# Part of a first product by Strassen's scheme, and one batch of attention input pooled in another layout, in a fused attention and MLP kernel

## The chip, the cores and the metric

One core of one Trainium2 chip. The metric is device time in microseconds (us) of one execution; several executions are timed and medians given. Every run here used one core. A profile gives one execution's span (its first to its last instruction), which in these runs is 1.7 to 2.9 us less than the time of that run.

## The reference, cut to what matters

```python
# q, k, v: (8 batches, 8 heads, 576, 64);  w_in: (512, 2048);  w_out: (2048, 512)
k_p = k.reshape(B, H, 72, 8, 64).mean(axis=3)          # pooled keys, v_p likewise
scores = (1/8) * q @ k_p^T ; attn = softmax(scores) ; a = attn @ v_p
x = a.transpose(0, 2, 1, 3).reshape(4608, 512)
h = x @ w_in ; g = h / (1 + exp(-h)) ; out = g @ w_out
```

## The kernel before

The 4608 tokens go through nine stages of 512. Stage t has a first product ("up", hidden values = w_in x) and a second ("down"). The attention of batch t + 1 is woven in: a list of fillers, each with a step number, is worked off between the matmuls. `spread` emits a filler once that many steps have been issued.

```python
def up(t, fillers, items):                       # 16 column groups g of 128
    step = spread(fillers, len(items) * KF)      # KF = 4
    for g, n0, n in items:
        hp_ps = ps_tile([128, 512], FP32, "mm", "hp_ps")      # 3 banks
        ...
            next(step)
            nc.tensor.matmul(hp_ps[:, r0:r1], lhsT=w_in_sb[:, kk, g*128:(g+1)*128], rhs=xT[...])
        nc.scalar.activation(h_T[:, g, n0:n0+n], hp_ps[:, :n], func=AF.Silu)
```

Strassen's scheme replaces the eight block products of a 2 x 2 block product by seven, at the price of extra sums. The second product is already done so (P, Q, R are PSUM tiles, the sums of hidden quarters and of weight quarters are made on the Vector engine). In the first two batches the pooling uses rows: partition = (head, position), which needs a small selection product afterwards. From batch 2 on it uses a tree over tiles with one position per partition.

```python
def slot_sums(name, j):        # rows: 128 partitions, 3 or 2 slots; used for batches 0 and 1
    ...                        # adds of 768, 384, 192 (or 512, 256, 128) elements
def select_v(b, a):            # brings pooled rows into place; both halves a use one PSUM tile
    if a == 0:
        st["v_ps"] = ps_tile([128, H, D], FP32, tag, "v_ps")
    ...
def copy_v(b, a):              # Vector: vp[:, half a] = v_ps[:, half a]
def tree(dsts, raw):           # one position per partition; 72 partitions busy
    ...
# in stage t, with a = t + 1:
f_up.append((0, lambda: pool_k(a)))
if t == 1:                     # batch 2: two half trees per tensor, no accumulating load
    f_up.append((46, lambda: pool_v(a, (0,))))
    f_down.append((30, lambda: pool_heads(a, "v", 1)))
elif t:
    f_up.append((10, lambda: pool_v(a)))
```

The softmax here doesn't subtract the row's maximum and nothing guards it: scores larger than these inputs give would overflow.

Of the kernel before, what the change touches and what calls it, by code (L numbers as in the profile page):

```python
# [27 lines left out]
FP32 = mybir.dt.float32  # L28
FP32R = mybir.dt.float32r
BF16 = mybir.dt.bfloat16  # L30
AX = mybir.AxisListType.X
AF = mybir.ActivationFunctionType
# [4 lines left out]
def kernel(  # L37
# [9 lines left out]
    nc = tc.nc  # L47
# [42 lines left out]
    def ps_tile(shape, dtype, tag, name):  # L90
        return psum.tile(shape, dtype, tag=tag, bufs=banks[tag], name=name)
# [18 lines left out]
    t_sb = singles.tile([128, 2, CQ], FP32, name="t_sb")  # L110
    xT = singles.tile([128, KF, NX], BF16, name="xT")


    kz = [singles.tile([128, 2, 2, SP], BF16, name=f"kz{n}") for n in range(2)]
    gate = singles.tile([128, 1], FP32, name="gate")
# [40 lines left out]
    def raw_tile(tag, heads, full=False):  # L156
        raw = big.tile([128, H * PH], FP32, tag=tag, name="raw")
        if full:
            return raw
        return raw[:SP, : H * PH].rearrange("k (h e) -> k h e", h=heads)  # L160

    def source(b, name):
        return (k if name == "k" else v)[b].rearrange("h (sp p) d -> sp h (p d)", p=POOL)


    def load_rows(eng, out, in_):
        for r0, r1 in ((0, 64), (64, SP)):
            eng.dma_start(out=out[r0:r1], in_=in_[r0:r1])

    def load_one(b, name):  # L170
        st = batches.setdefault(b, {})
        raw = raw_tile(f"{name}_raw", H)
        load_rows(nc.sync, raw, source(b, name)[:, :, :PH])
        st[f"{name}_raw"] = raw

# [43 lines left out]
    def pool_heads(b, name, i):  # L219
        tree([pooled(b, name, i)], batches[b][f"{name}_raws"][i])  # L220
# [21 lines left out]
    def k_transpose(b, parts=(0, 1)):  # L242
        st = batches[b]
        kT_ps = ps_tile([128, 2, 2, SP], BF16, "at", "kT_ps")
        for a in parts:
            for c in range(2):
# [18 lines left out]
    SA = SLOTS - 1  # L265
    row_tiles = {
        n: [
            raw_tile(f"{n}_raw{i}", H, full=True)[:, : m * RE].rearrange(
                "r (i e) -> r i e", e=RE
            ) for i, m in (("", SA), (2, SLOTS + 1 - SA))  # L270
        ] for n in "kv"
    }

# [62 lines left out]
    def copy_v(b, a, copy=nc.vector.tensor_copy):  # L336
        hs = slice(4 * a, 4 * (a + 1))
        copy(out=batches[b]["vp"][:, hs, :], in_=batches[b]["v_ps"][:SP, hs, :])
# [68 lines left out]
    def spread(fillers, n):  # L407
        todo = sorted(fillers, key=lambda f: f[0])
        for i in range(n):
            yield i  # L410
            while todo and todo[0][0] <= i:
                todo.pop(0)[1]()
        for f in todo:
            f[1]()


    def up(t, fillers, items):
        step = spread(fillers, len(items) * KF)
        for g, n0, n in items:
            hp_ps = ps_tile([128, 512], FP32, "mm", "hp_ps")  # L420
            c0 = (t * NTT + n0) % NX

            for r0, r1 in ((0, min(n, NX - c0)), (min(n, NX - c0), n)):
                for kk in range(KF) if r1 > r0 else ():
                    if r0 == 0:
                        next(step)
                    x0 = (c0 + r0) % NX
                    nc.tensor.matmul(  # L428
                        hp_ps[:, r0:r1],
                        lhsT=w_in_sb[:, kk, g * 128 : (g + 1) * 128],  # L430
                        rhs=xT[:, kk, x0 : x0 + r1 - r0],
                        start=(kk == 0), stop=(kk == KF - 1),
                    )
            nc.scalar.activation(h_T[:, g, n0 : n0 + n], hp_ps[:, :n], func=AF.Silu)  # L434
        for _ in step:
            pass

    def store(t, m, cs, engines=(nc.sync,)):
        n0 = (t * NTT + m * 128) // QP
# [220 lines left out]
    load_slots(nc.gpsimd, 1, "v", 4, 5)  # L660
    load_w_out(3)

    visits = [(f, g) for f in range(2) for g in range(2)]
    for t in range(NT):
        a = t + 1
        f_up, f_down = [], []
        if t == 0:
            GA = 11
            items = [(g, 0, HS) for g in range(GA)]
            items += [(g, HS, NTT - HS) for g in range(GA)]  # L670
            items += [(g, 0, NTT) for g in range(GA, KG)]
            f_up += [(1, lambda: denominators(0, 0, 1, on_dve=True))]
            f_up += [(5, lambda: denominators(0, 1, 1, on_dve=True))]
            f_up += [(13, lambda: numerators(0, 0, 1))]
            f_up += [(17, lambda: numerators(0, 1, 1))]
        else:
            items = [(g, 0, NTT) for g in range(KG)]
            for n, k0, k1, at in (
                (6, 0, 4, 20), (6, 4, 8, 36),
                (2, 0, 4, 51), (5, 0, 4, 52), (1, 0, 4, 53), (2, 4, 6, 58), (5, 4, 6, 59),  # L680
            ):
                f_up.append((at, lambda n=n, k0=k0, k1=k1: hidden_sum(n, k0, k1)))
            f_up.append((64, lambda: hidden_sum(2, 6, 8)))
            f_up.append((64, lambda: hidden_sum(5, 6, 8)))
            f_up.append((64, lambda: hidden_sum(1, 4, 8)))
            f_down.append((27 if t < NT - 1 else 41, lambda: hidden_sum(7, 0, 8)))

        for n, t0, f_to, at in (
            (1, 0, f_down, 48), (3, 0, f_down, 54), (4, 1, f_up, 12),
            (7, 1, f_down, 10), (6, 1, f_down, 50),  # L690
        ):
            for i in range(PW):
                if t == t0:
                    f_to.append((at + i, lambda n=n, i=i: weight_sum(n, i)))
        if a < B:
            q_at = [20, 28, 36, 44] if t else [82, 84, 86, 88]
            if t == 0:
                for j in range(2):
                    f_up.append((44 + 8 * j, lambda j=j: slot_sums("k", j)))
                    f_up.append((72 + 8 * j, lambda j=j: select_k(1, j)))  # L700
                    f_up.append((72 + 8 * j, lambda j=j: copy_k(1, j)))
                    f_down.append((20 + 10 * j, lambda j=j: slot_sums("v", j)))
                    f_down.append((37 + 3 * j, lambda j=j: select_v(1, j, "at")))
                    f_down.append((37 + 3 * j, lambda j=j: copy_v(1, j)))
            else:
                f_up.append((0, lambda: pool_k(a)))
                f_up.append((25, lambda: k_transpose(a)))
            for n in range(4):
                f_up.append((q_at[n], lambda n=n: q_transpose(a, n // 2, n % 2)))
            if t == 1:  # L710
                f_up.append((46, lambda: pool_v(a, (0,))))
                f_down.append((30, lambda: pool_heads(a, "v", 1)))
            elif t:
                f_up.append((10, lambda: pool_v(a)))
            if t == 0:
                f_down.append((0, lambda: load_q(2)))

                last = w_out_sb[:SP, KG - 1, d_model - 1 :]
                f_down.append(
                    (1, lambda: load_heads(2, "k", ("k_raw", "k_raw2"), last))  # L720
                )
                f_down.append(
                    (14, lambda: load_heads(2, "v", ("v_raw", "v_raw2"), last))
                )
            elif a + 1 < B:
                f_v = f_up if t > 1 else f_down
                f_up.append((0, lambda: load_q(a + 1)))
                f_up.append((1, lambda: load_one(a + 1, "k")))
                f_up.append((2, lambda: load_rest(a + 1, "k")))
                f_v.append((11 if t > 1 else 31, lambda: load_one(a + 1, "v")))  # L730
                f_v.append((12 if t > 1 else 32, lambda: load_rest(a + 1, "v")))
            f_down.append((0, attn_tables))

            if t:
                sc_at, den_at, nu_at = (1, 28, 56, 77), (28, 46, 69, 89), (46, 69, 89, 93)
            else:
                sc_at, den_at, nu_at = (1, 14, 22, 30), (14, 22, 30, 38), (42, 47, 52, 57)
            for n, (f, g) in enumerate(visits):
                f_down.append((den_at[n], lambda f=f, g=g: denominators(a, g, f)))
                f_down.append((sc_at[n], lambda f=f, g=g: scores(a, g, f)))  # L740


            for n, (f, g) in enumerate(visits):
                if n < 3 or not 3 <= t < B - 2:
                    f_down.append((nu_at[n], lambda f=f, g=g: numerators(a, g, f)))
                if n == 0 and 3 < t < B - 1:
                    f_down.append((nu_at[n], lambda: numerators(a - 1, 1, 1)))
        moe_tables()
        up(t, f_up, items)
        if t == 0:  # L750
            down(t, f_down, [(0, 1, 2), (3,)])
        else:
            down_quarters(t, f_down, last=t == NT - 1)
# [28 lines left out]
```

## Time and profile before

| | before |
|---|---|
| time, first 3 runs / all 4 of the first comparison | 295.84 / 295.86 us |
| span, granted clock | 294.7 us, 0.997 |
| Tensor / Vector / Scalar busy | 98 / 65 / 60 % |
| stage 1 (up start to next up start) | 54.21 to 86.02 = 31.8 us |
| stages 2 to 7 | 30.6, 30.1, 30.5, 30.3, 30.8, 26.0 us |

Stage ends are read off the chain of waits, where a run of `hp_ps` follows a run of 16 `o_psQ`. "Granted clock" is the share of its full clock that the Tensor engine got. A Vector sum of 512 elements per partition takes 0.68 us there in fp32 (`rr_sb`) and 0.42 in bf16 (`w_sum`). The prediction shows the lines that matter; two more serve for comparison. First the one Tensor wait in the middle of the kernel, from the view of waits (total us, times, longest), then, from the chain, the up of stage 7, which has no attention beside it:

```profile
PE sc_ps L348 <- DVE xT L396: 0.7, 1, 0.7
...
238.30 13.81 PE hp_ps L428 x64
```

### The profile page before, as it was taken

To read this page: it belongs to the slowest core of one execution; us is meant where nothing else is said; L and a number is where in the kernel's file an instruction comes from. 1 tells how busy PE (TensorE), PEld (TensorE's weight loads), DVE (VectorE), ACT (ScalarE), POOL (GpSimd) and SP (SyncE) were. 2 spreads that over 40 slices of the span, in tenths; PEclk is the share of its full clock that TensorE was granted. 3 is DMA by queue.
4 is the path that set the end of the run, shared out by engine and by line. 5 is a ranking of instruction groups with operands and counts; after the bars stand their busy time and mean duration, and the time that the engine had idled before them with its cause. 6 is when DMAs were issued, how large, how long until landed. Compare 5 with 4: busy or idle time off the path is not lost.

```text
span 294.7 us, 6052 instructions
## 1 busy us (share of the span) xinstructions
PE 287.9 (98%) x2417; PEld 175.6 (60%) x2417; DVE 191.2 (65%) x344; ACT 177.6 (60%) x366; POOL 42.8 (15%) x60
## 2 busy tenths in 40 slices
PE   8999999999999999999999999999999999999995
PEld 3348434446564666457788774476547654884584
DVE  4886445999978566865586659666865642741562
ACT  1677675567566865676667675776577666407500
POOL 8654100001300120013001710110000000000000
PEclk9999999999999999999999999999999999999998
DMA  7999999958794797487857895783500032004003
GB/s 215 271 282 205 247 229 180 209 147 174 106 177 108 160 132 136 106 177 111 150 128 162 120 122 137 167 116 51 123 20 2 2 89 53 2 22 117 6 12 135
DMA packets 34909, 37.65 MB, mean 128 GB/s; under 512 B 9856, under 2 KB 26368, under 8 KB 34880
## 3 DMA queue, kind: packets, MB, share of 16 engines
q0 software_dynamic: 20128, 18.50, 37.3%
q1 hardware_dynamic: 14176, 17.84, 26.5%
q10 hardware_dynamic: 576, 0.92, 0.9%
q8 instruction: 19, 0.31, 0.5%
q14 instruction: 10, 0.08, 0.1%
HBM read 36.70 MB, written 9.44 MB: 157 GB/s over the span
## 4 chain that ended last, share of the span: by engine, by line
PE 86%; DVE 10%; ACT 1%; issue 1%; DVEq 0%
PE hp_ps L428 37%; PE o_psQ L535 14%; PE o_psP L535 14%; PE o_psR L535 4%; PE sc_ps L348 4%; PE o_ps L462 4%; PE warm_ps L583 4%; PE nu_ps L388 3%; DVE raw L197 3%; DVE h_sum L495 2%; PE den_ps L365 2%; DVE w_sum L513 2%; DVE qT L148 1%; DVE xT L396 1%; PE kz_ps L313 1%
## 5 line engine op out<-in xcount | busy, mean ns | idle before, releaser
L428 PE MATMUL hp_ps<-xT,w_in_sb 128*128 128x512 bf16 (+3 forms) x684 | 128.2, 345 | 0.4 <-ACT h_T L434 0.4
L434 ACT ACTIVATE h_T<-hp_ps 128x512 bf16<-128x512 f32 (+2 forms) x155 | 87.4, 567 | 57.4 <-PE hp_ps L428 45.3
L428 PEld LDWEIGHTS <-w_in_sb 128*128 128x128 bf16 x684 | 65.9, 98 | 56.6 <-issue 1.5
L495 DVE TENSOR_TENSOR h_sum<-h_T 128x1024 bf16<-128x1024 bf16 (+2 forms) x88 | 52.0, 637 | 36.1 <-ACT h_T L434 36.1
L535 PEld LDWEIGHTS <-h_sum 128*128 128x128 bf16 x640 | 60.9, 98 | 15.1 <-issue 6.5
L356 ACT ACTIVATE es<-sc_ps 72x288 bf16<-72x288 f32 x128 | 41.4, 403 | 13.2 <-PE sc_ps L348 13.1
L396 DVE TENSOR_TENSOR xT<-nu_ps,rec 128x288 bf16<-128x288 f32 x64 | 25.7, 448 | 12.0 <-PE nu_ps L388 11.8
L535 PEld LDWEIGHTS <-h_T 128*128 128x128 bf16 x256 | 23.6, 98 | 6.5 <-issue 4.1
L177 POOL DMA_DIRECT2D raw<-in_k_dram x5 | 7.1, 1420 | 114.5 <-DVE h_sum L495 48.4
L148 DVE STREAM_TRANSPOSE qT<-q_bf 128x576 bf16<-128x576 bf16 x32 | 23.6, 758 | 0.0
L374 ACT ACTIVATE lnd<-den_ps 128x288 f32<-128x288 f32 x30 | 12.3, 411 | 16.6 <-PE nu_ps L388 9.8
L197 DVE TENSOR_TENSOR raw<-raw 72x1024 f32<-72x1024 f32 (+1 forms) x18 | 19.7, 1094 | 0.1
L291 DVE TENSOR_TENSOR raw<-raw 128x768 f32<-128x768 f32 (+3 forms) x16 | 10.5, 654 | 11.1 <-DMA raw<-in_v_dram 7.8
L535 PE MATMUL o_psP<-w_out_sb,h_sum 128*128 128x256 bf16 x128 | 17.6, 273 | 0.0
L535 PE MATMUL o_psQ<-w_out_sb,h_sum 128*128 128x256 bf16 x128 | 17.6, 273 | 0.0
L535 PE MATMUL o_psQ<-w_sum,h_T 128*128 128x256 bf16 x128 | 17.5, 274 | 0.0
L535 PE MATMUL o_psP<-w_sum,h_sum 128*128 128x256 bf16 x128 | 17.0, 273 | 0.5 <-DVE o_sb L556 0.5
L535 PE MATMUL o_psP<-w_sum,h_T 128*128 128x256 bf16 x128 | 16.5, 273 | 0.0
L535 PE MATMUL o_psR<-w_sum,h_sum 128*128 128x256 bf16 x128 | 16.5, 273 | 0.0
L462 PE MATMUL o_ps<-w_out_sb,h_T 128*128 128x512 bf16 x64 | 15.9, 381 | 0.0
L535 PE MATMUL o_psQ<-w_sum,h_sum 128*128 128x256 bf16 x128 | 15.4, 273 | 0.0
L348 PE MATMUL sc_ps<-qT,kz 32*72 32x288 bf16 x256 | 14.4, 295 | 0.9 <-DVE xT L396 0.7
(58 smaller groups left out, 212.0 us busy)
## 6 DMA issues: line engine op xcount, KB each, us to landing
out_dram<-o_sb SPq DMA_DIRECT2D x128, 64.0 KB, 1.7
raw<-in_k_dram SPq DMA_DIRECT2D x8, 512.0 KB, 5.2
raw<-in_v_dram SPq DMA_DIRECT2D x7, 512.0 KB, 6.9
q_bf<-in_q_dram POOLq DMA_DIRECT2D x6, 576.0 KB, 11.8
raw<-in_k_dram POOLq DMA_DIRECT2D x5, 576.0 KB, 9.1
raw<-in_v_dram POOLq DMA_DIRECT2D x5, 576.0 KB, 9.9
w_in_sb<-in_moe_w_in_dram POOLq DMA_DIRECT2D x8, 256.0 KB, 8.5
w_out_sb<-in_moe_w_out_dram POOLq DMA_DIRECT2D x4, 512.0 KB, 13.7
```

Source lines behind the costliest of these rows:

```text
L148: nc.vector.transpose(out=st["qT"][:, a, f * QF : (f + 1) * QF].rearrange("r i c p -> r (i c p)"), in_=st["q_bf"][:, a, f * n : (f + 1) * n],)
L197: nc.vector.tensor_add(out=raw[:, :, :w], in0=raw[:, :, :w], in1=raw[:, :, w : 2 * w])
L348: nc.tensor.matmul(sc[s], lhsT=kz[b % 2][rows, g, c, :], rhs=st["qT"][rows, g, f * QF : (f + 1) * QF, c, :], start=(c == 0), stop=(c == 1),)
L356: nc.scalar.activation(es[:, s, :], sc[s], func=AF.Exp, scale=score_scale)
L374: nc.scalar.activation(lnd, den_ps[:, :HS], func=AF.Ln)
L396: nc.vector.tensor_mul(out=xT[:, 2 * g + c, cols], in0=nu[c][:, :HS], in1=rec)
L428: nc.tensor.matmul(hp_ps[:, r0:r1], lhsT=w_in_sb[:, kk, g * 128 : (g + 1) * 128], rhs=xT[:, kk, x0 : x0 + r1 - r0], start=(kk == 0), stop= ...
L434: nc.scalar.activation(h_T[:, g, n0 : n0 + n], hp_ps[:, :n], func=AF.Silu)
L462: nc.tensor.matmul(ps, lhsT=h_T[:, g, m * 128 : (m + 1) * 128], rhs=w_out_sb[:, g, :], start=(g == 0), stop=(g == KG - 1),)
L495: nc.vector.tensor_tensor(out=h_sum[n][:, ks, :], in0=quarter(*a, ks), in1=quarter(*b, ks), op=op)
L535: nc.tensor.matmul(ps[b][:, c, :], lhsT=left(n, kt, c), rhs=W_OUT[n][:, kt, :], start=b not in begun, stop=kt == KQ - 1, skip_group_check= ...
L583: nc.tensor.matmul(warm_ps, lhsT=warm[:, :128], rhs=warm, start=True, stop=True)
```

## The change

The intent was to take Tensor time out of the up of stages 1 to 8, and to pay for it with Vector time. Four of the 16 column groups become seven products of 256 x 256 x 256 blocks. To make room on the Vector engine, batch 2 is pooled as rows, the value sums move from up to down, and two of four query transposes do too.

```diff
+            items = (
+                G(0, 1, 2, 3) + ["2", "5", "1"] + G(8) + ["4", "3"] + G(9) + ["7", "6"]
+                + G(10) + ["6s"] + G(11, 12, 13, 14, 15)
+            )
+            for n in U_X:
+                f_up.append((0, lambda n=n: unit_x_sum(t, n)))     # 5 bf16 sums of x
...
+            if it == "2":
+                product(2, "P", True)
+                nc.scalar.copy(r_sb, ps["P"])
+            elif it == "5":
+                product(5, "Q", True)
+                tt(out=rr_sb, in0=ps["Q"], in1=r_sb, op=ALU.add)
+            elif it == "1": ...                                    # t_sb, then 4, 3, 7, 6
...
-            q_at = [20, 28, 36, 44] if t else [82, 84, 86, 88]
+            q_at = [31, 2, 39, 30] if t else [82, 84, 86, 88]      # odd ones in down
+            elif t == 1:
+                for j in range(2):
+                    f_up.append((21 + 4 * j, lambda j=j: select_k(2, j)))
+                    f_up.append((21 + 4 * j, lambda j=j: copy_k(2, j)))
+                    f_down.append((8 + 10 * j, lambda j=j: slot_sums("v", j)))
+                    f_down.append((40 + j, lambda j=j: select_v(2, j, "at")))
+                    f_down.append((40 + j, lambda j=j: copy_v(2, j)))
             else:
                 f_up.append((0, lambda: pool_k(a)))
+                f_down.append((10, lambda: pool_v(a)))
...
             if t == 0:
+                f_down.append((0, load_batch_2))                   # keys, queries: Pool queue
+                f_down.append((31, load_values_2))
+                for n in U_W:
+                    f_down.append((12, lambda n=n: unit_weight_sum(n)))
+                for j in range(2):
+                    f_down.append((43 + 7 * j, lambda j=j: slot_sums("k", j)))
```

More of the change, by code (lines that the diff above doesn't have):

```diff
@@ L111 @@
     xT = singles.tile([128, KF, NX], BF16, name="xT")
+    w_sum1 = singles.tile([128, 5, 2, 256], BF16, name="w_sum1")
+    x_sum = singles.tile([128, 5, 2, NQ], BF16, name="x_sum")
+    c_sb = [singles.tile([128, 2, NQ], FP32, name=f"c_sb{n}") for n in range(2)]
     kz = [singles.tile([128, 2, 2, SP], BF16, name=f"kz{n}") for n in range(2)]
@@ L168, in load_rows, with load_one @@
             eng.dma_start(out=out[r0:r1], in_=in_[r0:r1])
-    def load_one(b, name):
+    def load_one(b, name, behind=None):
         st = batches.setdefault(b, {})
         raw = raw_tile(f"{name}_raw", H)
+        if behind is not None:
+            nc.gpsimd.tensor_copy(out=raw[:, 0, :1], in_=behind)
         load_rows(nc.sync, raw, source(b, name)[:, :, :PH])
@@ L267 @@
         n: [
-            raw_tile(f"{n}_raw{i}", H, full=True)[:, : m * RE].rearrange(
+            big.tile([128, m, RE], FP32, tag=f"{n}_raw2", name="raw") if i else
+            raw_tile(f"{n}_raw", H, full=True)[:, : m * RE].rearrange(
                 "r (i e) -> r i e", e=RE
-            ) for i, m in (("", SA), (2, SLOTS + 1 - SA))
+            ) for i, m in enumerate((SA, SLOTS + 1 - SA))
         ] for n in "kv"
@@ L414, in spread @@
             f[1]()
-    def up(t, fillers, items):
-        step = spread(fillers, len(items) * KF)
-        for g, n0, n in items:
-            hp_ps = ps_tile([128, 512], FP32, "mm", "hp_ps")
-            c0 = (t * NTT + n0) % NX
-            for r0, r1 in ((0, min(n, NX - c0)), (min(n, NX - c0), n)):
-                for kk in range(KF) if r1 > r0 else ():
-                    if r0 == 0:
-                        next(step)
-                    x0 = (c0 + r0) % NX
+    UL, UH = 4, 6
+    UW = {
+        (i, j): w_in_sb[:, 2 * j : 2 * j + 2, 128 * u : 128 * (u + 2)]
+        for i, u in enumerate((UL, UH)) for j in range(2)
+    }
@@ new lines, with x_quarter, unit_weight_sum @@
+    U_W = {2: ((1, 0), (1, 1)), 5: ((0, 0), (0, 1)), 1: ((0, 0), (1, 1)),
+           6: ((1, 0), (0, 0)), 7: ((0, 1), (1, 1))}
+    U_X = {1: ((0, 0), (1, 1)), 4: ((1, 0), (0, 0)), 3: ((0, 1), (1, 1)),
+           7: ((1, 0), (1, 1)), 6: ((0, 0), (0, 1))}
+    U_WI = {n: i for i, n in enumerate(U_W)}
+    U_XI = {n: i for i, n in enumerate(U_X)}
+    def x_quarter(t, i, j):
+        c0 = (t * NTT + j * NQ) % NX
+        return xT[:, 2 * i : 2 * i + 2, c0 : c0 + NQ]
+    def unit_weight_sum(n):
+        a, b = U_W[n]
+        nc.vector.tensor_tensor(
+            out=w_sum1[:, U_WI[n]], in0=UW[a], in1=UW[b],
+            op=ALU.subtract if n in (6, 7) else ALU.add,
+        )
@@ new lines, in unit_x_sum, with unit_weights, unit_x @@
+    def unit_x_sum(t, n):
+        a, b = U_X[n]
+        nc.vector.tensor_tensor(
+            out=x_sum[:, U_XI[n]], in0=x_quarter(t, *a), in1=x_quarter(t, *b),
+            op=ALU.subtract if n in (3, 4) else ALU.add,
+        )
+    def unit_weights(n):
+        if n in U_WI:
+            return w_sum1[:, U_WI[n]]
+        return UW[0, 0] if n == 3 else UW[1, 1]
+    def unit_x(t, n):
+        if n in U_XI:
+            return x_sum[:, U_XI[n]]
+        return x_quarter(t, 0, 0) if n == 2 else x_quarter(t, 1, 1)
@@ L428, in up, with product @@
+    def up(t, fillers, items):
+        step = spread(
+            fillers,
+            sum(KF if isinstance(it, tuple) else 2 * (it != "6s") for it in items),
+        )
+        ps = {}
+        def product(n, bank, first):
+            if first:
+                ps[bank] = ps_tile([128, 2, NQ], FP32, "at", f"u_ps{bank}")
+            w, x = unit_weights(n), unit_x(t, n)
+            for u in range(2):
+                next(step)
+                for kk in range(2):
                     nc.tensor.matmul(
-                        hp_ps[:, r0:r1],
@@ L430, in up @@
-                        lhsT=w_in_sb[:, kk, g * 128 : (g + 1) * 128],
-                        rhs=xT[:, kk, x0 : x0 + r1 - r0],
-                        start=(kk == 0), stop=(kk == KF - 1),
-                    )
-            nc.scalar.activation(h_T[:, g, n0 : n0 + n], hp_ps[:, :n], func=AF.Silu)
+                        ps[bank][:, u, :], lhsT=w[:, kk, 128 * u : 128 * (u + 1)],
+                        rhs=x[:, kk, :], start=first and u == 0 and kk == 0,
+                        stop=kk == 1, skip_group_check=True,
+                    )
@@ new lines, in hidden @@
+        def hidden(i, j, src):
+            g = (UL, UH)[i]
+            nc.scalar.activation(
+                h_T[:, g : g + 2, j * NQ : (j + 1) * NQ], src, func=AF.Silu
+            )
+        tt = nc.vector.tensor_tensor
+        for it in items:
+            if it == "2":
[4 more added lines that the diff above has]
+                tt(out=rr_sb, in0=ps["Q"], in1=r_sb, op=ALU.add)
+            elif it == "1":
+                product(1, "R", True)
+                tt(out=t_sb, in0=ps["R"], in1=rr_sb, op=ALU.subtract)
+            elif it == "4":
+                product(4, "P", False)
+                hidden(1, 0, ps["P"])
+            elif it == "3":
+                product(3, "Q", False)
+                hidden(0, 1, ps["Q"])
+            elif it == "7":
+                product(7, "P", False)
+                tt(out=c_sb[0], in0=ps["P"], in1=t_sb, op=ALU.add)
+                hidden(0, 0, c_sb[0])
+            elif it == "6":
+                product(6, "Q", False)
+                tt(out=c_sb[1], in0=ps["Q"], in1=t_sb, op=ALU.add)
+            elif it == "6s":
+                hidden(1, 1, c_sb[1])
+            else:
+                plain(t, step, *it)
@@ L435, in up, with plain @@
         for _ in step:
             pass
+    def plain(t, step, g, n0, n):
+        hp_ps = ps_tile([128, 512], FP32, "mm", "hp_ps")
+        c0 = (t * NTT + n0) % NX
+        for r0, r1 in ((0, min(n, NX - c0)), (min(n, NX - c0), n)):
+            for kk in range(KF) if r1 > r0 else ():
+                if r0 == 0:
+                    next(step)
+                x0 = (c0 + r0) % NX
+                nc.tensor.matmul(
+                    hp_ps[:, r0:r1],
+                    lhsT=w_in_sb[:, kk, g * 128 : (g + 1) * 128],
+                    rhs=xT[:, kk, x0 : x0 + r1 - r0],
+                    start=(kk == 0), stop=(kk == KF - 1),
+                )
+        nc.scalar.activation(h_T[:, g, n0 : n0 + n], hp_ps[:, :n], func=AF.Silu)
@@ L661, with load_batch_2, load_values_2 @@
     load_w_out(3)
+    def load_batch_2():
+        load_slots(nc.gpsimd, 2, "k", 0, 3)
+        load_slots(nc.gpsimd, 2, "k", 3, 4)
+        load_slots(nc.gpsimd, 2, "k", 4, 5)
+        load_q(2)
+    def load_values_2():
+        load_slots(nc.gpsimd, 2, "v", 0, 3)
+        load_slots(nc.gpsimd, 2, "v", 3, 4)
+        load_slots(nc.gpsimd, 2, "v", 4, 5)
     visits = [(f, g) for f in range(2) for g in range(2)]
@@ L676 @@
         else:
-            items = [(g, 0, NTT) for g in range(KG)]
+            G = lambda *gs: [(g, 0, NTT) for g in gs]
+            items = (
+                G(0, 1, 2, 3) + ["2", "5", "1"] + G(8) + ["4", "3"] + G(9) + ["7", "6"]
+                + G(10) + ["6s"] + G(11, 12, 13, 14, 15)
+            )
+            for n in U_X:
+                f_up.append((0, lambda n=n: unit_x_sum(t, n)))
             for n, k0, k1, at in (
-                (6, 0, 4, 20), (6, 4, 8, 36),
+                (6, 0, 4, 20), (6, 4, 8, 46),
                 (2, 0, 4, 51), (5, 0, 4, 52), (1, 0, 4, 53), (2, 4, 6, 58), (5, 4, 6, 59),
@@ L707 @@
                 f_up.append((25, lambda: k_transpose(a)))
+                f_down.append((10, lambda: pool_v(a)))
             for n in range(4):
-                f_up.append((q_at[n], lambda n=n: q_transpose(a, n // 2, n % 2)))
-            if t == 1:
-                f_up.append((46, lambda: pool_v(a, (0,))))
-                f_down.append((30, lambda: pool_heads(a, "v", 1)))
-            elif t:
-                f_up.append((10, lambda: pool_v(a)))
-            if t == 0:
-                f_down.append((0, lambda: load_q(2)))
-                last = w_out_sb[:SP, KG - 1, d_model - 1 :]
-                f_down.append(
-                    (1, lambda: load_heads(2, "k", ("k_raw", "k_raw2"), last))
-                )
-                f_down.append(
-                    (14, lambda: load_heads(2, "v", ("v_raw", "v_raw2"), last))
-                )
+                f_to = f_down if t and n % 2 else f_up
+                f_to.append((q_at[n], lambda n=n: q_transpose(a, n // 2, n % 2)))
+            if t == 0:
+                f_down.append((0, load_batch_2))
[4 more added lines that the diff above has]
+                    f_down.append((43 + 7 * j, lambda j=j: slot_sums("k", j)))
             elif a + 1 < B:
-                f_v = f_up if t > 1 else f_down
                 f_up.append((0, lambda: load_q(a + 1)))
@@ L729 @@
                 f_up.append((2, lambda: load_rest(a + 1, "k")))
-                f_v.append((11 if t > 1 else 31, lambda: load_one(a + 1, "v")))
-                f_v.append((12 if t > 1 else 32, lambda: load_rest(a + 1, "v")))
+                f_down.append((11, lambda: load_one(a + 1, "v")))
+                f_down.append((12, lambda: load_rest(a + 1, "v")))
             f_down.append((0, attn_tables))
@@ L744 @@
                 if n < 3 or not 3 <= t < B - 2:
-                    f_down.append((nu_at[n], lambda f=f, g=g: numerators(a, g, f)))
+                    at = nu_at[n] + 2 * (t == 1 and n == 0)
+                    f_down.append((at, lambda f=f, g=g: numerators(a, g, f)))
                 if n == 0 and 3 < t < B - 1:
```

## The prediction

> **What bounds the kernel now.** I read the page first, then the chain of waits in order of time, then one table of busy time by stage, then the Vector and Tensor timelines of the places that table pointed to. A stage t is one tile of 512 tokens: a first product ("up", line 428), then a second product ("down", line 535; line 462 in stage 0), with the next batch's attention interleaved. The page:
>
> ```profile
> PE 287.9 (98%) x2417; PEld 175.6 (60%) x2417; DVE 191.2 (65%) x344; ACT 177.6 (60%) x366; POOL 42.8 (15%) x60
> ...
> PE 86%; DVE 10%; ACT 1%; issue 1%; DVEq 0%
> ```
>
> The Tensor engine sets the end, so a matmul removed is worth its own length. But a tenth of the chain is Vector work, and the chain in order of time shows where it lies (columns: start, length, what):
>
> ```profile
> 49.52 0.39 PE nu_ps L388 x8
> 50.32 0.45 DVE xT L396
> 50.77 0.62 DVE w_sum L513 x2
> ...
> 76.29 0.68 DVE rr_sb L550
> 76.97 0.38 DVE xT L396
> 77.39 0.40 PE sc_ps L348 x5
> ...
> 116.58 5.61 PE hp_ps L428 x26
> 122.32 8.20 PE hp_ps L428 x38
> 130.75 0.37 PE sc_ps L348 x8
> ...
> 144.93 1.75 PE o_psQ L535 x16
> 146.67 5.46 PE hp_ps L428 x50
> ```
>
> From 50.3 to 77.4 us every link is Vector work: stage 1 is where both engines are full. Later stages are Tensor alone. Two prices are in these lines: 64 matmuls of 512 columns take 5.61 + 8.20 = 13.81 us, 215.8 ns each; 16 of 256 columns take 1.75 us, 109.2 ns each. By stage (columns: stretch, its length, then busy us and count of PE, PEld, DVE, ACT, POOL):
>
> ```profile
> 54.20:68.30 14.10, 14.10 (x69) 6.39 (x68) 13.89 (x24) 10.61 (x17) 0.00 (x0) 1.00 0.73 160
> 68.30:86.00 17.70, 17.03 (x194) 12.01 (x193) 15.53 (x33) 11.66 (x27) 3.63 (x3) 1.00 0.91 155
> 86.00:99.80 13.80, 13.80 (x69) 6.30 (x67) 11.27 (x18) 8.96 (x15) 0.00 (x0) 1.00 0.64 148
> 99.80:116.40 16.60, 16.60 (x193) 11.82 (x192) 9.65 (x18) 11.66 (x27) 3.54 (x3) 1.00 0.81 130
> ```
>
> Rows one and two are stage 1: Vector has 0.2 us free in up and 2.2 in down. Rows three and four are stage 2: 2.5 and 7.0 us free. Stage 1's down loses about 1 us of Tensor time; nothing else does until the tail.
>
> [...] the trace's Vector order is the program's order everywhere that I looked. [...] The trace agrees: with 512 elements per partition, 0.69 us for fp32 and 0.42 for bf16 (start to start about 0.60 and 0.34, as consecutive ones overlap). [...]
>
> **The change, part by part.**
>
> Matmuls. In stages 1 to 8, 16 matmuls of 512 columns (3.45 us) become 7 x 2 x 2 = 28 of 256 (28 x 0.1092 = 3.06). Gain 0.39 us a stage, 3.2 us in all (1.1%): this is the ceiling, as the three other engines cannot shorten a stage bound by Tensor.
>
> Steady stages (2 to 8). Added on Vector in up: five bf16 sums of x (5 x 0.34 = 1.7 us) and four fp32 evictions (4 x 0.60 = 2.4). Moved out of up to down: value sums (1.9) and two query transposes (1.4). Scalar gets one more copy of 0.6 against 0.27 us of slack per group of 0.86. Walking through up from its start: x sums end at +2.4, key sums at +4.3, the first Strassen product starts at +3.45 (after four plain groups), its Scalar copy ends at +4.9, the two sums follow by +6.7; the accumulating products need P and Q at +7.7 and +8.15, when Scalar has let go at +7.2 and +7.8. No stall. In down, Vector finishes the hidden sums at +2.1, then transpose 0.7, values 1.9, r_sb 0.6, a hidden sum 1.2, transpose 0.7, rr_sb 0.6: +7.8 where before it was about +6. The first numerators' products follow at +8.1 and +8.5 (in stages 4 to 6 also +8.9), and the third score visit, at +8.1 to +8.4, wants the bank that one of them frees. I take a stall of 0.1 us in stages 2 and 3 and 0.35 in 4 to 6, none in 7 and 8, which have no attention. Net: 2 x 0.3 + 3 x 0.05 + 2 x 0.39 = 1.5 us gained.
>
> Stage 0's down. Batch 2's keys as pooled rows are summed at steps 43 and 50 of 64. The same shapes for batch 1 show the price, the two halves taking 1.55 + 0.31 and 1.14 + 0.25 us, 3.2 together:
>
> ```profile
> 40.12 1.55 DVE L291 TENSOR_TENSOR raw<-raw 128x768 f32<-128x768 f32 x2 [7.20 <-DMA raw<-in_v_dram]
> 41.71 0.36 DVE L295 TENSOR_TENSOR v<-raw 128x192 bf16<-128x192 f32 x1
> 41.98 1.14 DVE L291 TENSOR_TENSOR raw<-raw 128x512 f32<-128x512 f32 x2
> 43.16 0.29 DVE L295 TENSOR_TENSOR v<-raw 128x128 bf16<-128x128 f32 x1
> ...
> 48.35 0.82 DVE L396 TENSOR_TENSOR xT<-nu_ps,rec 128x288 bf16<-128x288 f32 x2 [0.45 <-PE nu_ps L388]
> ...
> 52.75 1.42 DVE L513 TENSOR_TENSOR w_sum<-w_out_sb 128x512 bf16<-128x512 bf16 x4
> 54.09 0.81 DVE L396 TENSOR_TENSOR xT<-nu_ps,rec 128x288 bf16<-128x288 f32 x2
> ```
>
> The last line writes the x that stage 1's first group reads, and Tensor starts that group at 54.21: just in time. With the new order, from 48.35: four pairs of products 3.0, eight weight sums 2.7, one output copy 0.6, key sums 3.2, so 9.5 us, and the last pair ends at 57.85. The first group ends at 58.1 in place of 55.07: **3.0 us lost**. (The five weight sums at step 12, 1.7 us, fall into the idle 7.2 us before 40.12 and are free.)
>
> Stage 1's up. Less the 0.39, plus key selection on Tensor (0.2 + 0.57 us and two switches of about 0.1) in place of transposes of 0.36: +0.3. Vector has caught up. Down starts at 71.7, against 68.31.
>
> Stage 1's down. The numerators at step 48 need the values: hidden sums to +2.1, then transpose 0.7, value sums 1.9, weight sums 1.35, value sums 1.4, r_sb 0.6, hidden sum 1.15, transpose 0.7, rr_sb 0.6, value copy 0.35, which makes +10.8, where Tensor is there at +7.8. **About 3 us lost**, part of it already at the value selection. The stall of before (0.67 us, ending at 77.39) shrinks to 0.2, and the added selection on Tensor lies inside the wait. Stage 1 then ends near 92.7 in place of 86.02: +6.7.
>
> Sum: 295.84 + 6.7 - 1.5 = 301.0. I call 300.6, leaning a little to the other side since such a schedule was surely made to gain.
>
> **The rivals.**
> (a) The gain arrives whole: 3.2 us plus the 1 us of stage 1, about 292. For it: row cost is lower than the old trees (two trees of 4.5 us become 6.4 in all). Against it: Vector's total up to stage 1's numerators still grows, -9.0 for the trees, +6.4 for rows, +4.1 for Strassen, +0.7 for value copies and about +0.4 for key copies, and it had nothing left.
> (b) The wait goes to a transfer: batch 2's keys on the Pool queue land late. Before, the last weight block was issued at 28.77 and had landed at 43.6, and the queries issued behind it at 30.37 landed 15.8 us later, 2.6 after the weights. Keys of twice the bytes written but the same bytes read should land by about 47, ahead of 49.1. A miss by 3 us would give 303 to 304.
> (c) A clock drop from two stalls near 3 us: [...] so 302 to 304.
> (d) The steady stall is absent, the sums at the start of stage 1 as computed: 299.7. Or it doubles: 302.
>
> **Range and chances.** The two Vector sums of stage 1 are order and measured durations, so I trust 5 to 8 us there; the rest is -0.5 to -2.8. That gives 298 to 303.3, my 80% range. The line of 2% is 301.8; rivals b and c and the upper part of d lie beyond it. Faster by 2% (289.9) is under the ceiling of Tensor work: 0.01. Within 2%: 0.70. Slower: 0.29.
>
> **What would show it.** In the changed profile: the window of up in stages 7 and 8 shorter by 0.39 us; Tensor idle 2.5 to 3.5 us at the first hp_ps of stage 1, released by the Vector engine's xT; again 2 to 4 us in stage 1's down ahead of v_ps and nu_ps, released by the v sums or vp; Vector continuously busy from 48 to 61 us; steady stages shorter by 0 to 0.4. Wrong if stage 1 shows no Vector release of either kind, if those waits name a transfer, if the clock falls below 1 there, or if up in stages 7 and 8 isn't shorter.

## More of the kernel before

In the trace of this kernel, 340 Vector operations, 349 Scalar operations and 2417 matmuls start in the order in which the built program has them, without exception (420, 357 and 2529 in the changed kernel).

Every matmul of this kernel writes a PSUM tile (`ps_tile`).

## The result, and the profile after

| | before | after |
|---|---|---|
| time | 295.86 us (295.78 to 296.62) | 307.5 us (306.11 to 309.14) |
| ratio | | 1.039, 95% interval 1.032 to 1.046 |
| profiled span, granted clock | 294.7, 0.997 | 306.2, 0.983 |
| stage 1 ends at | 86.02 | 99.34 |
| stages 2 to 7 | 30.6, 30.1, 30.5, 30.3, 30.8, 26.0 | 30.2, 29.7, 30.5, 30.4, 30.9, 25.6 |

A ratio is the mean time of one kernel's runs over that of the other's in the same rounds, so it is not quite the ratio of the medians. The change made the kernel slower by 3.9%. By the end of stage 1 it is 13.3 us late; from there to the end it gains 1.8.

The page of the changed kernel: the Tensor share falls, and the clock row, nines up to its last slice before, has two dents, at slices of 7.7 us (the first near 60 us, the second near 88).

```profile
PE 292.3 (95%) x2529; PEld 185.9 (61%) x2529; DVE 223.7 (73%) x424; ACT 178.1 (58%) x374; POOL 46.1 (15%) x62
...
PEclk9999999799959999999999999999999999999999
```

Its view of Tensor waits, cut to those of stage 1:

```profile
PE v_ps L338 <- DVE vp L345: 4.7, 1, 4.7
PE hp_ps L532 <- DVE xT L403: 2.4, 2, 1.3
...
PE kz_ps L320 <- DVE kz L327: 0.8, 1, 0.8
```

All three name the Vector engine; no transfer is among them. The Tensor timeline (start, length, what, idle before and who ended it) puts them in time, and the Vector timeline shows what stood in front:

```profile
55.42 0.74 PE L532 MATMUL hp_ps<-xT,w_in_sb 128*128 128x512 bf16 x2 [1.12 <-DVE xT L403]
57.49 4.85 PE L532 MATMUL hp_ps<-xT,w_in_sb 128*128 128x512 bf16 x14 [1.33 <-DVE xT L403]
...
84.81 0.65 PE L338 MATMUL v_ps<-v,shifts 128*72 128x64 bf16 x6 [4.67 <-DVE vp L345]
```

```profile
49.01 1.54 DVE L298 TENSOR_TENSOR raw<-raw 128x768 f32<-128x768 f32 x2
...
56.98 0.82 DVE L403 TENSOR_TENSOR xT<-nu_ps,rec 128x288 bf16<-128x288 f32 x2
...
83.09 0.77 DVE L152 STREAM_TRANSPOSE qT<-q_bf 128x576 bf16<-128x576 bf16 x1
83.79 0.65 DVE L652 TENSOR_TENSOR rr_sb<-o_psQ,r_sb 128x512 f32<-128x512 f32 x1
84.36 0.40 DVE L345 CAST vp<-v_ps 72x256 bf16<-72x256 f32 x1
```

The key sums run at 49.01 without a wait, so the keys had landed. They push the last x product to 56.98, where before it ran at 54.09. The third matmul of stage 1 then starts at 57.49 in place of about 54.64: 2.85 us. Its 14 companions take 4.85 us, 346 ns each instead of 216. That is a slow clock and no wait. The table by stretch (length, busy us and count of PE, PEld, DVE, ACT and POOL, then PEclk, DMA share, GB/s) says so:

```profile
57.50:62.20 4.70, 4.70 (x15) 1.75 (x15) 3.41 (x10) 1.79 (x3) 0.00 (x0) 0.64 0.63 155
...
80.00:84.80 4.80, 0.15 (x3) 0.00 (x0) 4.69 (x9) 0.25 (x1) 0.00 (x0) 1.00 0.53 123
84.80:90.00 5.20, 5.18 (x37) 2.56 (x40) 3.05 (x8) 0.85 (x2) 2.17 (x2) 0.50 0.46 63
90.00:92.00 2.00, 2.00 (x17) 1.22 (x18) 0.20 (x1) 1.30 (x4) 0.00 (x0) 0.60 1.12 180
```

After each of the two long waits the clock is low for a while. Cut at its steps, the record is 0.50 from 57.5 to 60.9 and from 84.8 to 91.6 us, so for 3.4 and for 6.8 us, and 1.00 after each. By the table, 4.70 x (1 - 0.64) + 5.20 x 0.50 + 2.00 x 0.40 = 5.1 us of Tensor time lost while Tensor looks fully busy. So my theory after reading was: the predicted order effect in stage 1, plus two things that the prediction lacked, a clock drop after waits and a PSUM tile that ties the second half of a selection to the copy of the first. The rivals were that Strassen's own Vector work carries the loss, that stage 1 simply has too much Vector work for any order, and that the clock record is a by-product of the waits.

### The profile page after: what moved, and what is told of

Read it like the earlier page. It is cut to its first block, busy times and chain, and to the rows that moved or that the text cites. A ratio compares the mean times of both kernels' runs of the same rounds, so it can differ in the third digit from the quotient of the medians.

```text
span 306.2 us, 6366 instructions
## 1 busy us (share of the span) xinstructions
PE 292.3 (95%) x2529; PEld 185.9 (61%) x2529; DVE 223.7 (73%) x424; ACT 178.1 (58%) x374; POOL 46.1 (15%) x62
## 4 chain that ended last, share of the span: by engine, by line
PE 87%; DVE 9%; issue 2%; ACT 2%; DVEq 0%
PE hp_ps L532 32%; PE o_psQ L637 13%; PE o_psP L637 13%; PE o_psR L637 4%; PE sc_ps L355 4%; PE warm_ps L685 3%; PE u_psP L480 3%; PE u_psQ L480 3%; PE o_ps L564 3%; PE nu_ps L395 2%; PE den_ps L372 2%; DVE raw L298 2%; DVE xT L403 2%; DVE w_sum L615 1%; DVE rr_sb L652 1%
## 5 line engine op out<-in xcount | busy, mean ns | idle before, releaser
L532 PE MATMUL hp_ps<-xT,w_in_sb 128*128 128x512 bf16 (+3 forms) x540 | 105.5, 347 | 2.8 <-DVE xT L403 2.4
L538 ACT ACTIVATE h_T<-hp_ps 128x512 bf16<-128x512 f32 (+2 forms) x123 | 68.3, 557 | 53.3 <-PE hp_ps L532 40.4
L532 PEld LDWEIGHTS <-w_in_sb 128*128 128x128 bf16 x540 | 52.5, 98 | 43.9 <-issue 5.2
L381 ACT ACTIVATE lnd<-den_ps 128x288 f32<-128x288 f32 x30 | 12.3, 410 | 23.7 <-PE den_ps L372 13.7
L152 DVE STREAM_TRANSPOSE qT<-q_bf 128x576 bf16<-128x576 bf16 x32 | 24.3, 767 | 0.2 <-DMA q_bf<-in_q_dram 0.2
L298 DVE TENSOR_TENSOR raw<-raw 128x768 f32<-128x768 f32 (+3 forms) x24 | 15.6, 651 | 9.7 <-DMA raw<-in_v_dram 6.2
L480 PEld LDWEIGHTS <-w_sum 128*128 128x128 bf16 x160 | 15.7, 98 | 4.8
L637 PE MATMUL o_psP<-w_sum,h_T 128*128 128x256 bf16 x128 | 18.2, 289 | 0.0
L637 PE MATMUL o_psR<-w_sum,h_sum 128*128 128x256 bf16 x128 | 17.5, 279 | 0.0
L355 PE MATMUL sc_ps<-qT,kz 32*72 32x288 bf16 x256 | 15.6, 299 | 0.5 <-DVE qT L152 0.3
```

The lines of the kernel that those rows point to most:

```text
L152: nc.vector.transpose(out=st["qT"][:, a, f * QF : (f + 1) * QF].rearrange("r i c p -> r (i c p)"), in_=st["q_bf"][:, a, f * n : (f + 1) * n],)
L298: nc.vector.tensor_add(out=raw[..., :w], in0=raw[..., :w], in1=raw[..., w : 2 * w])
L355: nc.tensor.matmul(sc[s], lhsT=kz[b % 2][rows, g, c, :], rhs=st["qT"][rows, g, f * QF : (f + 1) * QF, c, :], start=(c == 0), stop=(c == 1),)
L381: nc.scalar.activation(lnd, den_ps[:, :HS], func=AF.Ln)
L480: nc.tensor.matmul(ps[bank][:, u, :], lhsT=w[:, kk, 128 * u : 128 * (u + 1)], rhs=x[:, kk, :], start=first and u == 0 and kk == 0, stop=kk ...
L532: nc.tensor.matmul(hp_ps[:, r0:r1], lhsT=w_in_sb[:, kk, g * 128 : (g + 1) * 128], rhs=xT[:, kk, x0 : x0 + r1 - r0], start=(kk == 0), stop= ...
```

## The experiments

Each edit is against the kernel named. Each call timed the kernel before again on its chip; its medians were 296.18, 296.37 and 296.45 us in the three calls. All results were correct.

### Keeping Tensor busy in the waits (keep_warm, warm_first)

```diff
 # the changed kernel, in the plain first product
+        if t == 1 and g == 0:
+            for _ in range(15):     # zeros, into the tile that the real first matmul writes
+                nc.tensor.matmul(hp_ps, lhsT=warm[:, :128], rhs=warm, start=True, stop=True)
 # in select_v; keep_warm only
+        if b == 2 and a == 1:
+            busy_ps = ps_tile([128, 512], FP32, "at", "busy_ps")
+            for _ in range(20):
+                nc.tensor.matmul(busy_ps, lhsT=warm[:, :128], rhs=warm, start=True, stop=True)
```

> The changed kernel with matmuls on zeros put into its two long Tensor waits of stage 1 (15 before the first group, 20 before the second half of the value selection), results never read. Clock theory: the waits of 2.4 and 4.7 us stay as long but the clock stays at full speed after them, so the windows that ran at 0.64 for 4.7 us and at 0.50 to 0.60 for 7.2 us run at 1.0: 1.7 + 2.6 + 0.8 = about 5 us come back, to 302. Rival (the time lies in the waits alone, the clock record is a by-product): the waits are unchanged, so 306 to 309 as the changed kernel.

Measured: 304.26 us (303.87 to 304.51), ratio 1.027 (1.025 to 1.029), clock 0.999 to 1.0 in every run. The waits are filled and the work behind them runs at the normal pace (16 matmuls in 3.62 us):

```profile
57.84 3.62 PE L539 MATMUL hp_ps<-xT,w_in_sb 128*128 128x512 bf16 x16
...
83.93 0.48 PE L342 MATMUL v_ps<-v,shifts 128*72 128x64 bf16 x6 [0.35 <-DVE vp L349]
```

The clock theory stands, as useless work made the kernel faster. The gain is 3.2 us from the median and 4.9 from the profiled run of 309.14. I had expected 302, taking the 5 us of the profiled run off the median of all runs, but the changed kernel's runs differ in how many slow stretches they catch: clock 0.989 at 306.1 and 306.2 us, 0.983 at 308.8 and 309.1. (One stretch of 3.4 us at 0.50 is 1.7 us, 0.006 of the span, so by this estimate 0.994, 0.989 and 0.983 are one, two and three.)

> The changed kernel with the zero matmuls in the first wait only. The clock stays full up to the second wait and drops after it: about 1.7 us better than the changed kernel's 309 runs, 307, with a single stretch of low clock of 3.4 or 6.8 us after the value selection. If low clock after the second wait is a late effect of the first, it is absent here too: 304.

Measured: 305.53 us (305.19 to 306.71), ratio 1.032 (1.030 to 1.035). The second drop comes without the first, so it is no late effect of it. The time is lower than the 307 that I expected, as the profiled run caught a single slow stretch after the value wait (clock 0.62 over 4 us) where the changed kernel's profiled run caught a double one (0.50 over 6.8 us).

### A tile for each half (two_banks)

```diff
 # the changed kernel
-        if a == 0:
+        if a == 0 or b == 2:
             st["v_ps"] = ps_tile([128, H, D], FP32, tag, "v_ps")     # kz_ps likewise
```

> The changed kernel with each half of batch 2's key and value selection in a PSUM tile of its own. Shared-tile theory: the 0.8 us wait at the second key selection and the 4.7 us wait at the second value selection, both released by the copy of the first half, go; the Vector queue still brings the values at the same time, so the numerators wait instead, about 3 us: 1.5 to 2.5 us better, more if the shorter wait spares a part of the low clock. Rival (the Vector queue alone sets it): unchanged within 0.5 us, the wait moves whole to the numerators.

Measured: 304.77 us (302.31 to 305.07), ratio 1.027 (1.023 to 1.031): 2.7 us better by the medians. The 4.7 us wait splits into one for the sums themselves and one for the copy that the numerators read, 3.0 together, and the 0.8 us wait at the keys is gone:

```profile
PE nu_ps L396 <- DVE vp L346: 1.7, 1, 1.7
PE v_ps L339 <- DVE v L302: 1.5, 2, 1.3
```

(The second line's 1.5 contains 0.2 from stage 0.) Three microseconds at the values is what the prediction had computed, and the numerators start 10.8 us into the second product (81.84 from 71.03), as it had said; the shared tile made the wait 4.7. Not all of the 2.7 us is the tile, though. At the same clock of 0.989 two_banks takes 304.7 to 305.1 us against 306.1 and 306.2, 1.3 less. Its profiled run (302.31, clock 0.994) has one slow stretch less: the clock held after the first wait, 1.33 us as in the changed kernel, where 14 matmuls then took 4.85 us:

```profile
56.91 3.33 PE L533 MATMUL hp_ps<-xT,w_in_sb 128*128 128x512 bf16 x14 [1.33 <-DVE xT L404]
```

With the clock held on both sides (keep_warm against both_undone, below) the tiles are worth 2.9 us; the waits themselves say 4.7 + 0.8 - 3.0 = 2.5. In the changed kernel's trace Tensor writes the second half (84.81) only after Vector has read the first (84.36, for 0.40 us); why the two are kept in this order is not shown.

### One part alone (strassen_only, rows_only)

```diff
 # strassen_only: the changed kernel with batch 2 loaded and pooled as before
-            elif t == 1: ... slot_sums, select_k, select_v of batch 2     # loads: cut here
+                if t == 1:
+                    f_up.append((46, lambda: pool_v(a, (0,))))
+                    f_down.append((30, lambda: pool_heads(a, "v", 1)))
 # rows_only: the changed kernel without Strassen (its sums of x and of weights go too)
-            items = (G(0, 1, 2, 3) + ["2", "5", "1"] + ...)
+            items = G(*range(KG))
```

> Strassen in stages 1 to 8 and the value sums in the second product, but batch 2 loaded and pooled as in the kernel before. If the pooled rows carry the loss: stage 1 costs 3 to 4 us more than before (4.1 us of Strassen work on a Vector engine that had nothing free), stages 2 to 8 give 1.8 back: 297 to 299, no low clock. If Strassen's Vector work carries it: 303 or more.

> The changed kernel with the plain first product in every stage; batch 2 as pooled rows, value sums in the second product. If the rows carry the loss: 3 us at the start of stage 1, 3 to 5 us at its values, and the low clock after both (5 us), nothing given back later: 306 to 309. If Strassen carries it: 297 to 300, since the rows are less Vector work than the trees.

Measured: strassen_only 302.81 us (299.68 to 302.86), ratio 1.019 (1.013 to 1.024, so whether it is slower by 2% is unclear); rows_only 309.37 us (308.79 to 309.69), ratio 1.044 (1.042 to 1.046). The rows, with the value sums and transposes moved along with them, cost as much as the whole change and more, since they take no Strassen gain back. They do so with less Vector work than the kernel before (189.7 us busy against 191.2 over the whole kernel), so it is not the amount. But Strassen alone is not harmless either: put on stage 1's full Vector queue it makes new waits,

```profile
PE sc_ps L354 <- DVE xT L402: 2.2, 1, 2.2
PE u_psQ L479 <- DVE rr_sb L498: 1.3, 1, 1.3
...
PE kT_ps L253 <- DVE kp L214: 1.2, 1, 1.2
```

and I had expected no clock drop there, which was wrong: with no wait longer than 2.2 us, the profiled run has 0.50 from 64.2 to 66.2 us and 0.54 from 83.7 to 87.0. Its four runs show the price by themselves: 299.68 us at clock 1.0, and 302.76 to 302.86 at 0.986 to 0.989. The run without drops lies 0.7 above the range of 297 to 299 that I had for the waits; the drops add 3.1, which brings the median to 0.2 from the 303 that was to speak for Strassen's own Vector work. So that work costs in stage 1 too: the one run at full clock is 3.5 us over the kernel before, even after what the later stages give back.

### The kernel before with idle Vector work (before_delay)

```diff
 # the kernel before
+            if t == 0:
+                for at in (43, 43, 43, 50, 50):
+                    f_down.append((at, lambda: nc.vector.memset(t_sb, 0.0)))
```

> The kernel before with five useless fills of 128x512 fp32 on the Vector engine (0.55 to 0.6 us each, 2.9 us together) at the steps of stage 0 where the changed kernel sums batch 2's keys; nothing else. Order theory: the first group of stage 1 starts 2.7 to 3 us later and the stage never makes it up, as Vector had no slack: +2.8 us, and with the low clock after the wait [...] another 1 to 1.8: 299.5 to 300.5. Rival (Vector catches up within stage 1): 297 or less.

Measured: 300.33 us (298.88 to 300.81), ratio 1.013 (1.010 to 1.015). The fills take 0.48 us each with gaps between, and move the last x product from 54.09 to 57.02, much as the key sums did. That reproduces the changed kernel's first wait and its clock drop with no other part of the change present:

```profile
55.46 0.74 PE L428 MATMUL hp_ps<-xT,w_in_sb 128*128 128x512 bf16 x2 [0.81 <-DVE xT L396]
57.52 4.80 PE L428 MATMUL hp_ps<-xT,w_in_sb 128*128 128x512 bf16 x13 [1.33 <-DVE xT L396]
```

The clock is 0.64 from 57.2 to 62.0. Again the runs sort by clock: 298.88 at 1.0, 300.26 to 300.81 at 0.994. One drop costs 1.4 to 1.9 us, and nothing in the program decides whether it comes, as these are runs of one program.

### Both missing terms taken away at once (both_undone)

The changed kernel with the tiles of two_banks and zero matmuls in the three waits that are left (15 before the first group, 5 before the second value selection, 7 before batch 2's first numerators).

> The changed kernel without the two things that the prediction left out: halves of the selections in PSUM tiles of their own (as two_banks), and matmuls on zeros in the three waits that are left (15, 5 and 7), so that the clock holds. If these two are all that was missing, the prediction's own sum stands here: 301.0 within 0.7 us, clock 1.0, and stage 1 ends 6.7 us later than before within 0.7. If something else is missing: 302.5 or more.

Measured: 301.4 us (300.93 to 301.76), ratio 1.017 (1.015 to 1.018), clock 0.999 to 1.0. The prediction's own sum was 301.0, or 5.2 us more than before; this is 5.0 more than the kernel before of its call. Stage 1 ends at 91.99, 6.0 us later than before, just under the 6.7 within 0.7 that I expected. Nothing else of size is missing. By the medians, holding the clock gives 3.2 us (keep_warm) and the tiles then another 2.9.

### The same work in another order (reordered)

```diff
 # two_banks, with
-    f_down (stage 0): slot_sums("k", j) at 43 + 7 * j
+    f_up (stage 1):   slot_sums("k", j) at 0
-    stage 1: weight sums 4 at up 12, 7 at down 10, 6 at down 50; hidden sum 7 at 27; q transpose at 30
+    stage 1: weight sums 4 at up 40, 7 at down 66, 6 at down 82; hidden sum 7 at 72; q transpose at 58
+    stages 2 to 6: hidden sum 7 at 50
```

> The changed kernel with all its work, in another order on the Vector queue: key sums of batch 2 from the end of stage 0 to the start of stage 1, weight sums 4, 7 and 6, hidden sum 7 and one transpose of stage 1 to just ahead of their readers, selections in tiles of their own, hidden sum 7 later in stages 2 to 6. Order theory (sums stand ahead of evictions that Tensor waits for): no wait over 0.5 us in stage 1, full clock, 293.5 to 295.5. Amount theory (stage 1 has more Vector work than fits): the waits come back elsewhere in stage 1, 297 or more.

Measured: 295.18 us (294.92 to 295.98), ratio 0.997 (0.995 to 0.999), clock 0.999 to 1.0. No Vector work was taken away (424 instructions as in the changed kernel, 222.6 us busy against 223.7), and 12 us went, 1.4 of them in stages 4 to 6 (late_h7, below, has that move alone) and about 2.7 with the tiles. One wait is left in stage 1, longer than the 0.5 us that I had allowed:

```profile
PE o_psP L638 <- DVE h_sum L598: 0.8, 1, 0.8
```

So the amount of Vector work is not what lost the time; its place in the queue is. My rival (a) in the prediction and my own argument against it ("it had nothing left") both counted amounts.

### Strassen where there is room (late_strassen, late_h7)

```diff
 # strassen_only, with
+            if t == 1:
+                items = G(*range(KG))       # stage 1 as in the kernel before, its fillers too
 # late_h7, also
-            f_down.append((27 if t < NT - 1 else 41, lambda: hidden_sum(7, 0, 8)))
+            f_down.append((27 if t in (1, NT - 2) else 50 if t < NT - 1 else 41,
+                           lambda: hidden_sum(7, 0, 8)))
```

> Stages 0 and 1 exactly as in the kernel before (apart from five weight sums in an idle stretch of stage 0); Strassen, the value sums in the second product and the moved transposes from stage 2 on. If the loss of the change lies wholly in stage 1: the 1.8 us that stages 2 to 8 gave in the changed kernel remain and nothing is paid, 294.0, full clock throughout. Rival (Strassen itself hurts once the Tensor queue is in step, through its extra evictions): 296 or more.

> As late_strassen, with the hidden sum for product 7 moved from step 27 to step 50 of the second product in stages 2 to 6, so that 1.15 us of Vector work no longer stands ahead of rr_sb and the numerators' products. If those stand in the way of the third score visit in stages 4 to 6 (which gained nothing): 3 x 0.4 us come back, 292.8. Rival (the stages 4 to 6 lose it elsewhere): as late_strassen, 294.0.

Measured, five rounds: late_strassen 294.69 us (294.44 to 295.01), ratio 0.994 (0.993 to 0.996); late_h7 293.62 us (293.13 to 293.96), ratio 0.991 (0.989 to 0.992). Both are faster than both kernels, by 0.6% and 0.9% than the one before, which is clear of the noise. Against the kernel before of the same rounds (296.37) that is 1.7 and 2.75 us; in microseconds I had set the two 0.7 to 0.8 too low, part of it because the kernel before ran 0.5 us longer on this chip. Moving one 1.2 us sum by 23 steps gives what the stages 4 to 6 lacked. The chain has the start of stage 4 and, in its last line here, of stage 7:

```profile
146.17 3.49 PE hp_ps L531 x32
...
236.56 3.45 PE hp_ps L531 x16
```

Stages 4 to 6 take 90.4 us, against 91.6 in the kernel before (146.67 to 238.30) and 91.8 in the changed kernel (159.18 to 250.97).

## Why the prediction was wrong

It gave 300.6 us, 298.0 to 303.3, with 0.29 for slower by over 2%; it came to 307.5. Two steps failed, about equal in size: the wait at stage 1's values was put too short, because a shared tile was overlooked, and the clock was left out of the sum. One of its own signs of being wrong came: the clock fell below 1 in stage 1. Point by point:

- **Ceiling of 0.39 us a stage: right.** Stage 7's up, 13.81 us before, ends at 264.38 from 250.97, 13.41.
- **Steady stages, 1.5 us gained: near, 1.8, in part by luck.** Stages 2 and 3 gained 0.4 each (0.3 predicted), 4 to 6 lost 0.03 to 0.07 each (0.05 gained predicted), 7 gained 0.4 and the last 0.8, half of it in its final stores, which the prediction did not have; the stall of the third score visit by the Vector queue was real there, as late_h7 shows by removing it.
- **Stage 0's key sums, 3.0 us: right.** 2.85 us, released by xT as named, and reproduced by before_delay.
- **Stage 1's up, +0.3: right.** In two_banks, whose clock held there in the profiled run, it is 14.1 us from the third matmul to the second product (56.91 to 71.03) against 13.7 before (54.64 to 68.31), 0.4 more.
- **The sum of stage 1, +6.7: a slip.** Its terms as written give 3.0 + 0.3 + 3.0 - 0.5 = 5.8; both_undone has 6.0.
- **Stage 1's values, "About 3 us lost": the first step that failed.** The sum over the queue was right, and two_banks shows it as 1.3 + 1.7. But "the added selection on Tensor lies inside the wait" failed: the second half of the selection waits for the copy of the first, 4.7 us, and 0.8 more at the keys by the same tie. I had listed banks for the scores and numerators and not for the selections.
- **The clock: the second step that failed.** It stood as rival (c), 302 to 304, and outside the sum; no trace had shown its size then. The drop was not a side case: every timed run of the changed kernel has it (0.983 or 0.989), with 5.1 us lost in the profiled one and 3.2 us of the median returned by keep_warm. In the profiled run the first slow stretch cost 1.7 us (3.4 us at 0.50). I did not see that after the wait of 4.7 us it can be twice as long (6.8 us at 0.50), nor that the waits of 1.12 and 1.33 us at the first product are enough (in before_delay 0.81 and 1.33 us, with two matmuls between them).
- **Rival (b), late keys: did not happen.** The sums at 49.01 did not wait.
- **The argument against (a): wrong in kind.** It held that Vector's total had no room. The total fits (reordered); the order did not.

Both missing terms undone give 301.4, 6.1 us less than the changed kernel's median, so the two explain the error. What decides whether a given wait is followed by a low clock is not settled: in runs of the same program it is and it isn't.

## What to carry to other kernels

Adding work to an engine with free time cost nothing here only where each piece lay behind the evictions and copies that the bound engine waits for (reordered: the same work, 12 us less than the changed kernel). So write down, for each piece, the step by which its reader needs it, and place it there, not where its input is ready. In before_delay 2.1 us of waits on the Tensor engine brought 1.4 to 1.9 us more where the clock dropped after them; my estimate from that run is that such a wait should be priced at up to twice its length. Compare runs by granted clock before explaining spread. A saving that only some stages can afford is worth having in those stages alone (late_h7: 0.9% faster than before, the whole change 3.9% slower).
